# Sink values loaded late, and x of batches 2 to 4 transposed by the DMA crossbar in place of TensorE

## The chip, the cores and the metric

The kernel runs on one core of a Trainium2 chip. The metric is the device time of one execution in microseconds; smaller is better. A core has TensorE (PE: matmuls into PSUM, with weight loads that overlap them), VectorE (DVE), ScalarE (ACT), GpSimd (POOL) and SyncE (SP), which here only issues transfers. SyncE's transfers go through a hardware queue (q1 in the profile), GpSimd's through a software queue (q0); 16 DMA engines serve both. Each engine runs its instructions in their written order and waits on semaphores.

## The reference

An attention layer whose heads are of two kinds, followed by a wave-like mixing layer. B is 4, H 8, S 768, D 64, so the model width is 512; 4 sink positions, a window of 64.

```
scores = q @ k.T / sqrt(D)                       # per batch and head, 768 x 768
retrieval heads (0, 2, 6): causal mask
streaming heads (1, 3, 4, 5, 7): causal and (key < 4 or query - key < 64)
x = softmax(scores) @ v                          # (B, S, 512), heads side by side
theta = x @ w_theta
y = w_tok_r @ (x * cos(theta)) + w_tok_i @ (x * sin(theta))
u = x + y
out = u + relu(u @ w_ch)
```

## The kernel before, in words

All matmuls run in bf16. A batch has an attention part and a mixing part. Attention: q and k of head pairs are transposed on TensorE (`turn_qk`, line 251) and copied to SBUF by ScalarE or VectorE (`keep_qk`); scores S go to PSUM (`multiply`, line 322), ScalarE takes the exponential into P or, for streaming heads, P_st (lines 338 to 349), VectorE masks P_st (line 358) and GpSimd the diagonal blocks of P. The value matmuls (`values`, line 409, tile pav) of a block row i of 128 queries multiply these with v (tile vt), with a copy of v that is shifted by half a block (vx), and with the values of the sinks (vs). A column of ones in each gives the softmax sum, and `normalize` (VectorE, lines 414 and 416) writes a row of x.

Mixing: x is transposed four blocks at a time on TensorE (`turn_x`, line 421) into PSUM and copied into xT (`keep_x`, line 424: ScalarE in batch 1, VectorE in batches 2 to 4). `theta` (line 432) multiplies xT with w_theta, ScalarE takes cosine and sine (`wave`, tiles ct and st), VectorE multiplies x with the cosine (`z_real`, tile zr, line 442) and GpSimd, or VectorE for part of batch 1, x with the sine (`z_imag`, zi, line 445). `mix` (line 455, tile py) applies w_tok_r and w_tok_i, `make_u`, `turn_u`, `keep_u`, `channel` (line 474, pc) and `finish` (line 478) make the output, and SP stores it (line 481).

Values reach the core through SP: `load_v` (line 218) loads a head pair in two transfers into one of four staging buffers st_v; `cast_v` (line 222) makes vt, `shift_v` (lines 228 and 229 in batch 1, 232 and 233 later) makes vx. The sink values come by `sink_values` (line 244), five transfers for two batches at a time into the one buffer vs_f, and a VectorE cast (line 698) into vs. GpSimd issues the loads of q, k and the weights, with a cast from float.

No loop sets the order of the instructions. Each piece of work is a `Step` with an engine, an assumed duration, the steps it comes after, and the buffer slots it takes and gives back. `Plan.order` simulates the steps with these numbers and emits them by their simulated start; an engine takes the ready step with the longest path behind it. So a changed cost or dependency may move instructions anywhere. Real waits come from the tiles that instructions read and write. The plan's slots of note: score banks "s" 2 (also taken by pav and theta), transposition banks "x" 2, staging "st_v" 4.

Of the kernel before, what the change touches and what calls it, by code (L numbers as in the profile page):

```python
# [31 lines left out]
class Plan:  # L32
# [3 lines left out]

    LATENCY = {"PE": (230, 0), "ACT": (190, 60), "DVE": (120, 60), "POOL": (150, 60), "SP": (50, 0), "DMA": (2000, 0)}
    SWITCH = {"PE": 95, "ACT": 1300}  # L40
    HOLD = {"PE": 1500, "ACT": 8000}

# [11 lines left out]
    def order(self, free):  # L54
# [4 lines left out]
        rank = {}  # L59
# [4 lines left out]
        ready_at = {id(s): 0 for s in self.steps}  # L64
# [16 lines left out]
        while events:  # L81
            now = events[0][0]
            while events and events[0][0] <= now:
                _, _, done = heapq.heappop(events)
                if done is not None:
                    for g in done.give:
                        holding[id(g)] -= 1
                        if holding[id(g)] == 0:
                            slots[g.take] += 1
            for e in engines:  # L90
                if free.get(e, 0) > now:
                    continue
                best = None
                for s in ready.get(e, ()):
                    if ready_at[id(s)] > now or (s.take and slots[s.take] < 1):
                        continue
                    value = -ready_at[id(s)] if e == "DMA" else rank[id(s)] + s.bias
                    if s.mode and s.mode != mode.get(e):
                        value -= self.HOLD.get(e, 0)
                    if best is None or value > best[0]:  # L100
                        best = (value, s)
                if best is None:
                    continue
                s = best[1]
                ready[e].remove(s)
                t = now
                if s.mode and s.mode != mode.get(e):
                    if mode.get(e):
                        t += self.SWITCH.get(e, 0)
                    mode[e] = s.mode  # L110
                if s.take:
                    slots[s.take] -= 1
                s.start, s.end = t, t + s.ns
                out.append(s)
                lat = self.LATENCY[e]
                free[e] = s.end
                heapq.heappush(events, (s.end, count, None))
                heapq.heappush(events, (s.end + lat[0], count + 1, s))
                heapq.heappush(events, (s.end + lat[1], count + 2, None))
                count += 3  # L120
                for n in later[id(s)]:
                    waiting[id(n)] -= 1
                    ready_at[id(n)] = max(ready_at[id(n)], s.end + lat[n.eng == e])
                    if waiting[id(n)] == 0:
                        ready.setdefault(n.eng, []).append(n)
                        heapq.heappush(events, (ready_at[id(n)], count, None))
                        count += 1
# [6 lines left out]
def kernel(  # L134
# [14 lines left out]
    nc = tc.nc  # L149
# [268 lines left out]
    def turn_x(b, i):  # L418
        pt = state["ptx", b, i] = ps_x.tile([128, 1024], BF16, tag="x", name="pt")
        for kk in range(KD):  # L420
            nc.tensor.transpose(pt[:, kk * 128:(kk + 1) * 128], state["x", b][:, i, kk * 128:(kk + 1) * 128], ident)  # L421

    def keep_x(b, i):
        (nc.scalar.copy if b == 0 else nc.vector.tensor_copy)(state["xT", b][:, :, i * 128:(i + 1) * 128], state.pop(("ptx", b, i))[:, :DM].rearrange("p (k t) -> p k t", k=KD))

# [117 lines left out]

    cleared = [add(eng, ns, lambda n=n: clear(n)) for n, (eng, ns) in enumerate((("DVE", 900), ("POOL", 1300), ("DVE", 600), ("POOL", 1300)))]
    landed = {}
    gate = [add("DMA", ns, None) for ns in (2600, 2400, 4800)]
    for n in range(4):
        for what in "qk":
            landed[what, 0, n] = gate[min(n, 2)]
# [36 lines left out]
    def v_steps(b):  # L586
        for n in range(4):
            if b == 0:
                issue = add("DVE", 200, lambda n=n: load_v(0, n, kT[n // 2]), [kept["k", 0, n // 2]], take="st_v")
                land = add("DMA", 2000, None, [issue])  # L590
            else:
                issue = add("SP", 1500, lambda b=b, n=n: load_v(b, n), [cast[b - 1, n], xk[b - 1, 5]], take="st_v")
                land = add("DMA", 2000, None, [issue])
            old = [s for key, s in av.items() if key[0] == b - 1] if b else [cleared[1]]
            cast[b, n] = add("DVE" if b == 0 else "POOL", 570 if b == 0 else 830, lambda b=b, n=n: cast_v(nc.gpsimd if b else nc.vector, b, n), [land] + old, give=[issue])
            for x, h in enumerate(PAIRS[n]):
                if not IS_RETR[h]:
                    shift[b, h] = add("POOL", 960, lambda b=b, n=n, x=x: shift_v(nc.gpsimd, b, n, x), [cast[b, n]], give=[issue])

    def attention_steps(b):  # L600
        got = {}
# [24 lines left out]
        for i in range(NB):  # L626
            need = [sunk[b][1], sink_done[b // 2]] if i else []
            n = 0
            for h in range(H):
                pn = [x for x in range(4) if h in PAIRS[x]][0]  # L630
                need.append(cast[b, pn])
                if IS_RETR[h]:
                    need += [got[h, j, i] for j in range(i + 1)]
                    n += i + 1
                else:
                    need += [got[h, None, i], shift[b, h]]
                    n += 3 if i else 2
            av[b, i] = add("PE", n * 31 + 30, lambda b=b, i=i: first_values(b, i), need, take="s", mode="128")
            old = [ud[b - 2, t] for t in range(NB)] if b > 1 else []
            norm[b, i] = add("DVE", 850, lambda b=b, i=i: normalize(b, i), [av[b, i]] + old, give=[av[b, i]])  # L640
            xt[b, i] = add("PE", 224, lambda b=b, i=i: turn_x(b, i), [norm[b, i]], take="x", mode="128")
            old = [th[b - 1, t, y] for t in (0, 2, 4) for y in range(2)] if b else []
            xk[b, i] = add("DVE" if b else "ACT", 400 if b else 480, lambda b=b, i=i: keep_x(b, i), [xt[b, i]] + old, give=[xt[b, i]])
        for i in (0, 2, 4):
            for y in range(2):
# [12 lines left out]
    def mlp_steps(b):  # L658
        for t in range(NB):
# [6 lines left out]
            ch[b, t] = add("PE", 864, lambda b=b, t=t: channel(b, t), [uk, channel_w], take="m", give=[uk], mode="128")  # L666
            fin = add("DVE", 680, lambda b=b, t=t: finish(b, t), [ch[b, t]], take="ot", give=[ch[b, t], ud[b, t]], bias=URGE)
            st = add("SP", 100, lambda b=b, t=t: store(b, t), [fin])
            add("DMA", 900, None, [st], give=[fin])

    turn_steps(0)
    v_steps(0)
# [19 lines left out]
    weights(4, 2, [])  # L692
    ones_done = add("POOL", 600, sink_ones, [cleared[3]])
    sink_done = []
    for half in range(2):
        first = add("SP", 500, lambda half=half: sink_values(2 * half), [cleared[2]] + sink_done)
        land = add("DMA", 100, None, [first])
        sink_done.append(add("DVE", 480, lambda half=half: nc.vector.tensor_copy(vs[:32, 2 * half:2 * half + 2, :, :D], vs_f), [land, cleared[3], ones_done]))
    attention_steps(0)
    for b in range(1, B):  # L700
        turn_steps(b)
        v_steps(b)
        if b + 1 < B:
            load_steps(b + 1, [kept[what, b - 1, n] for what in "qk" for n in range(4)])
        attention_steps(b)
        mlp_steps(b - 1)
# [46 lines left out]
```

## Time and profile before

| | us |
|---|---|
| median of 3 runs | 226.41 (226.37 to 229.37) |
| profiled execution | 229.25 |
| its span, first to last instruction | 227.5 |
| PE busy | 195.2 (86%) |
| DVE busy | 122.2 (54%) |
| ACT busy | 120.2 (53%) |
| POOL busy | 101.1 (44%) |

The profiled execution is one run, taken with the hardware profiler; durations below are its own. Views of the trace name an instruction by its source line, its engine and its tiles, and say how long an engine stood idle before it and what it waited for. A busy time by stretch adds up an engine's instructions in a piece of the span; PEclk is the granted clock of TensorE there. Where a stretch is full on one engine, work taken off it shortens the run; where it isn't, the wait that ends last counts.

### The profile page before, as it was taken

What the parts mean: (1) busy time and instruction counts of PE and PEld (TensorE: products, weight loads), DVE (VectorE), ACT (ScalarE), POOL (GpSimd) and SP (SyncE); (2) the same over time, 40 slices, a digit from 0 to 9 for tenths busy, and PEclk for the clock granted to TensorE, in tenths of its full rate; (3) what the DMA queues carried; (4) which work ended last, traced back from release to release, by engine and by line L of the source; (5) the groups of instructions that cost most, each with busy time, mean ns of one, the idle gap of its engine ahead of it and who ended that gap; (6) DMA issues with size and microseconds to landing.
All of it is one profiled execution on the core that took longest, in us unless ns stands there. A gap on an engine that the chain in (4) does not pass through costs nothing.

```text
span 227.5 us, 5040 instructions
## 1 busy us (share of the span) xinstructions
PE 195.2 (86%) x2124; PEld 113.1 (50%) x2124; DVE 122.2 (54%) x203; ACT 120.2 (53%) x156; POOL 101.1 (44%) x180
## 2 busy tenths in 40 slices
PE   0688549968997899999999999959999999689990
PEld 0555339634554577544553468525544575234440
DVE  6327815389542168479135168495451764974341
ACT  2477402793499960184777563644977526703120
POOL 7955992072488300349852200299835000780000
PEclk9999999999999589999999999997999999999997
DMA  6994599999994934902103000960012000210303
GB/s 76 164 210 108 80 174 213 192 200 199 195 209 98 202 55 118 208 14 81 49 0 127 14 0 3 242 178 0 3 48 94 3 3 0 92 49 0 138 0 140
DMA packets 39759, 22.63 MB, mean 99 GB/s; under 512 B 25912, under 2 KB 36664, under 8 KB 39736
## 3 DMA queue, kind: packets, MB, share of 16 engines
q0 software_dynamic: 11072, 9.70, 27.4%
q1 hardware_dynamic: 28664, 12.61, 21.2%
q8 instruction: 16, 0.26, 0.5%
q14 instruction: 7, 0.06, 0.1%
HBM read 25.71 MB, written 6.29 MB: 141 GB/s over the span
## 4 chain that ended last, share of the span: by engine, by line
PE 72%; DVE 8%; ACT 6%; DMA 5%; POOL 3%; issue 3%; POOLq 1%; SPq 1%; DVEq 0%; ACTq 0%
PE py L455 26%; PE pav L409 9%; PE ps L322 9%; PE pc L474 7%; PE pt L251 7%; PE ps L432 6%; DVE zr L442 5%; POOL zi L445 3%; PE pt L421 3%; PE pt L464 3%; DMA vs_f<-in_v_dram 2%; PE pt L494 2%; DMA kb<-in_k_dram 2%; ACT P L341 2%; ACT P_st L338 1%
## 5 line engine op out<-in xcount | busy, mean ns | idle before, releaser
L455 PE MATMUL py<-zr,wtokTr 128*128 128x512 bf16 x144 | 39.7, 385 | 6.3 <-DVE zr L442 6.3
L445 POOL TENSOR_TENSOR zi<-x,st 128x512 bf16<-128x512 bf16 x20 | 27.8, 1421 | 25.2 <-ACT st L439 19.8
L455 PE MATMUL py<-zi,wtokTi 128*128 128x512 bf16 x144 | 38.5, 379 | 0.1
L459 DVE TENSOR_TENSOR u<-x,py 128x512 bf16<-128x512 bf16 x24 | 16.5, 687 | 36.1 <-PE py L455 36.1
L322 PE MATMUL ps<-qT,kT 64*64 64x128 bf16 (+6 forms) x380 | 26.7, 266 | 6.5 <-ACT P L341 2.2
L442 DVE TENSOR_TENSOR zr<-x,ct 128x512 bf16<-128x512 bf16 x24 | 27.9, 1197 | 1.3 <-ACT ct L437 1.3
L468 ACT COPY uT<-pt 128x512 bf16<-128x512 bf16 x24 | 13.9, 586 | 26.5 <-PE pt L464 26.4
L478 DVE SCALAR_TENSOR_TENSOR ot<-pc,u 128x512 f32<-128x512 f32 x24 | 16.5, 688 | 16.4 <-PE pc L474 15.1
L222 POOL CAST vt<-st_v 128x768 bf16<-128x768 f32 x12 | 10.2, 856 | 33.3 <-DMA st_v<-in_v_dram 33.1
L322 PEld LDWEIGHTS <-kT 64*64 64x64 bf16 (+1 forms) x380 | 13.6, 113 | 21.7 <-issue 17.1
L200 POOL TENSOR_SCALAR_AFFINE_SELECT P<-P 128x256 bf16<-128x256 bf16 (+1 forms) x48 | 16.5, 365 | 17.2 <-ACT P L346 6.6
L474 PE MATMUL pc<-w_ch_sb,uT 128*128 128x512 bf16 x96 | 24.0, 380 | 0.0
L432 PE MATMUL ps<-w_theta_sb,xT 128*128 128x512 bf16 x96 | 23.2, 379 | 0.9 <-ACT st L439 0.9
L437 ACT ACTIVATE ct<-ps,half_pi 128x1024 f32<-128x1024 f32 x12 | 13.0, 1113 | 20.1 <-PE ps L432 19.5
L341 ACT ACTIVATE P<-ps 128x1024 bf16<-128x1024 f32 (+2 forms) x24 | 21.2, 923 | 4.5 <-PE ps L322 4.5
L455 PEld LDWEIGHTS <-wtokTr 128*128 128x128 bf16 x144 | 12.6, 98 | 19.7 <-issue 7.6
L258 ACT COPY qT<-pt 128x768 bf16<-128x768 bf16 x14 | 11.0, 802 | 18.7 <-PE pt L251 18.5
L455 PEld LDWEIGHTS <-wtokTi 128*128 128x128 bf16 x144 | 13.3, 98 | 14.9 <-issue 0.4
L358 DVE TENSOR_TENSOR P_st<-P_st,m_stream 128x512 bf16<-128x512 bf16 (+2 forms) x24 | 12.8, 543 | 14.7 <-ACT P_st L349 10.5
L409 PE MATMUL pav<-vx,P_st 128*128 128x65 bf16 x120 | 17.4, 207 | 3.5 <-POOL vx L228 3.5
L409 PE MATMUL pav<-vt,P 128*128 128x65 bf16 x252 | 16.1, 207 | 1.8 <-DVE x L416 1.8
L409 PE MATMUL pav<-vt,P_st 128*128 128x65 bf16 x120 | 17.5, 208 | 0.0
(73 smaller groups left out, 323.8 us busy)
## 6 DMA issues: line engine op xcount, KB each, us to landing
st_v<-in_v_dram SPq DMA_DIRECT2D x32, 192.0 KB
out_dram<-ot SPq DMA_DIRECT2D x24, 256.0 KB
qb<-in_q_dram POOLq DMA_DIRECT2D x3, 768.0 KB, 10.8
kb<-in_k_dram POOLq DMA_DIRECT2D x3, 768.0 KB, 15.4
wtok<-in_moe_w_tok_r_dram POOLq DMA_DIRECT2D x3, 384.0 KB, 11.9
wtok<-in_moe_w_tok_i_dram POOLq DMA_DIRECT2D x3, 384.0 KB, 12.7
w_theta_sb<-in_moe_w_theta_dram POOLq DMA_DIRECT2D x1, 512.0 KB, 5.7
w_ch_sb<-in_moe_w_ch_dram POOLq DMA_DIRECT2D x1, 512.0 KB, 21.1
```

The source lines that it names most:

```text
L200: nc.gpsimd.affine_select(out=t, in_=t, compare_op=ALU.is_ge, fill=0.0, base=base, pattern=pattern, channel_multiplier=cm)
L251: nc.tensor.transpose(pt[64 * x:64 * x + 64, j * 128:(j + 1) * 128], state[what, b][:, h, j * D:(j + 1) * D], ident)
L322: nc.tensor.matmul(ps[half, yy, c:c + w], l, r, start=True, stop=True, skip_group_check=True)
L341: nc.scalar.activation(P.rearrange("p (y c) -> p y c", y=2), ps[:, :, :w0], AF.Exp, scale=scale)
L409: nc.tensor.matmul(o, l, r, start=(m == 0), stop=True, skip_group_check=True)
L432: nc.tensor.matmul(ps[:, y], state["xT", b][:, kk, (i + y) * 128:(i + y + 1) * 128], w_theta_sb[:, kk], start=(kk == 0), stop=(kk == KD - 1))
L442: nc.vector.tensor_tensor(state["zr", b][:, i + y], state["x", b][:, i + y], state["ct", b, i][:, y], ALU.mult)
L445: (nc.vector if eng == "DVE" else nc.gpsimd).tensor_tensor(state["zi", b][:, i + y], state["x", b][:, i + y], state["st", b, i][:, y], ALU ...
L455: nc.tensor.matmul(py, wtokT[n][:, s, t * 128:(t + 1) * 128], z[:, s], start=(g == 0 and m == 0), stop=(g == 2 and m == 3))
L459: nc.vector.tensor_tensor(u, state["x", b][:, t], state.pop(("py", b, t)), ALU.add)
L474: nc.tensor.matmul(pc, uT[:, kk], w_ch_sb[:, kk], start=(kk == 0), stop=(kk == KD - 1))
L478: nc.vector.scalar_tensor_tensor(ot, state.pop(("pc", b, t)), 0.0, state.pop(("u", b, t)), ALU.max, ALU.add)
```

## The change

Three things change. The second half of the sink values (batches 3 and 4) is planned after the value loads of batch 2, and its load waits in the plan for the first cast of batch 2's values; before, both halves came at the start. In batches 2 to 4, `turn_x` and `keep_x` give way to one DMA transpose per block row, issued by SP (`send_x`: SBUF x, 128 x 512, to SBUF xT, four blocks of 128 x 128). In batch 1 the shifted copies vx are made by VectorE in place of GpSimd. With these, numbers of the plan change: the arrival of the first q and k loads, the cost of a value load and of a sink load on SP, and a separate DMA lane ("DMAH") for transfers that SP issues. Lines after the new function move by 3, later ones by up to 11 (698 becomes 705).

```diff
+    def send_x(b, i):
+        nc.sync.dma_start_transpose(state["xT", b][:, :, i * 128:(i + 1) * 128], state["x", b][:, i])
...
-    gate = [add("DMA", ns, None) for ns in (2600, 2400, 4800)]
+    gate = [add("DMA", ns, None) for ns in (4300, 2000, 6000)]
...
-                issue = add("SP", 1500, lambda b=b, n=n: load_v(b, n), [cast[b - 1, n], xk[b - 1, 5]], take="st_v")
-                land = add("DMA", 2000, None, [issue])
+                issue = add("SP", 700, lambda b=b, n=n: load_v(b, n), [cast[b - 1, n], xk[b - 1, 5]], take="st_v")
+                land = add("DMAH", 2000, None, [issue])
...
-                    shift[b, h] = add("POOL", 960, lambda b=b, n=n, x=x: shift_v(nc.gpsimd, b, n, x), [cast[b, n]], give=[issue])
+                    shift[b, h] = add("POOL" if b else "DVE", 960 if b else 340, lambda b=b, n=n, x=x: shift_v(nc.gpsimd if b else nc.vector, b, n, x), [cast[b, n]], give=[issue])
...
+            old = [th[b - 1, t, y] for t in (0, 2, 4) for y in range(2)] if b else []
+            if b:
+                issue = add("SP", 800, lambda b=b, i=i: send_x(b, i), [norm[b, i]] + old)
+                xk[b, i] = add("DMAH", 900, None, [issue])
+                continue
             xt[b, i] = add("PE", 224, lambda b=b, i=i: turn_x(b, i), [norm[b, i]], take="x", mode="128")
...
-    for half in range(2):
-        first = add("SP", 500, lambda half=half: sink_values(2 * half), [cleared[2]] + sink_done)
-        land = add("DMA", 100, None, [first])
-        sink_done.append(add("DVE", 480, lambda half=half: nc.vector.tensor_copy(vs[:32, 2 * half:2 * half + 2, :, :D], vs_f), [land, cleared[3], ones_done]))
+    def sink_steps(half, after):
+        first = add("SP", 1500, lambda: sink_values(2 * half), [cleared[2]] + after)
+        land = add("DMAH", 300, None, [first])
+        sink_done.append(add("DVE", 480, lambda: nc.vector.tensor_copy(vs[:32, 2 * half:2 * half + 2, :, :D], vs_f), [land, cleared[3], ones_done]))
+
+    sink_steps(0, [])
     attention_steps(0)
     for b in range(1, B):
         turn_steps(b)
         v_steps(b)
+        if b == 1:
+            sink_steps(1, [sink_done[0], cast[1, 0]])
```

What the plan makes of it is seen in the order of the instructions. SP's queue, from its start to the stores of batch 2 (vs_f is the sinks' buffer, st_v the staging of values, ot a result), before:

```order
L244 DMA vs_f<-in_v_dram 4x2x64 x5
L218 DMA st_v<-in_v_dram 128x6x64 x8
L244 DMA vs_f<-in_v_dram 4x2x64 x5
L218 DMA st_v<-in_v_dram 128x6x64 x8
L481 DMA out_dram<-ot 128x512 x3
L218 DMA st_v<-in_v_dram 128x6x64 x8
L481 DMA out_dram<-ot 128x512 x7
```

The same place after:

```order
L244 DMA vs_f<-in_v_dram 4x2x64 x5
L218 DMA st_v<-in_v_dram 128x6x64 x16
L244 DMA vs_f<-in_v_dram 4x2x64 x5
L424 DMA_TRANSPOSE xT<-x 128x4x128
L484 DMA out_dram<-ot 128x512 x2
L218 DMA st_v<-in_v_dram 128x6x64 x8
L424 DMA_TRANSPOSE xT<-x 128x4x128
L484 DMA out_dram<-ot 128x512
L424 DMA_TRANSPOSE xT<-x 128x4x128 x4
L484 DMA out_dram<-ot 128x512 x4
```

The second sink load now stands behind the value loads of batches 1 and 2, and transposes stand among stores and value loads.

On VectorE, the second cast of the sinks before, ahead of the first normalization of batch 1:

```order
L698 CAST vs<-vs_f 32x10x64
L222 CAST vt<-st_v 128x2x6x64
L358 TENSOR_TENSOR P_st<-P_st,m_stream 128x2x4x64 x2
L358 TENSOR_TENSOR P_st<-P_st,m_stream 128x4x64
L698 CAST vs<-vs_f 32x10x64
L414 RECIPROCAL r<-pav 128x8
L416 TENSOR_TENSOR x<-pav,r 128x2x4x64
```

And after, where it stands now, in the mixing part of batch 1:

```order
L445 TENSOR_TENSOR zr<-x,ct 128x512 x2
L448 TENSOR_TENSOR zi<-x,st 128x512 x3
L705 CAST vs<-vs_f 32x10x64
L501 COPY wtokTi<-pt 128x6x128
L358 TENSOR_TENSOR P_st<-P_st,m_stream 128x2x4x64
L462 TENSOR_TENSOR u<-x,py 128x512
```

It moved from before the first x to behind the last z products of batch 1.

On TensorE, scores of batch 2 (ps, with the numbers of the buffers) before:

```order
L322 MATMUL ps_1132<-qT0_88,kT0_92 128x128
L322 LDWEIGHTS kT0_92
L322 MATMUL ps_1141<-qT0_88,kT0_92 128x256
L322 LDWEIGHTS kT0_92
L322 MATMUL ps_1141<-qT0_88,kT0_92 128x256
L322 LDWEIGHTS kT1_93
L322 MATMUL ps_1147<-qT1_89,kT1_93 128x256
```

And after, the end of such a score tile:

```order
L322 MATMUL ps_1045<-qT0_88,kT0_92 128x256
L322 LDWEIGHTS kT0_92
L322 MATMUL ps_1045<-qT0_88,kT0_92 128x256
L458 LDWEIGHTS wtokTi_87
L458 MATMUL py_1012<-zi_463,wtokTi_87 128x512
```

Before, score tiles of batch 2 follow one another; after, token-mixing matmuls of batch 1 stand between them.

## Rows read from the trace of the kernel before

**Rows 1.** The page's busy time, share of the span and instructions, TensorE.

```profile
PE 195.2 (86%) x2124; PEld 113.1 (50%) x2124; DVE 122.2 (54%) x203; ACT 120.2 (53%) x156; POOL 101.1 (44%) x180
```

**Rows 2.** Busy time by stretch: length, engines' busy us (instructions), PEclk, DMA share, GB/s.

```profile
24.50:34.60 10.10, 4.77 (x53) 3.45 (x52) 4.89 (x11) 1.28 (x2) 9.65 (x16) 1.00 0.95 153
34.60:40.50 5.90, 5.90 (x93) 5.90 (x94) 3.00 (x8) 1.45 (x3) 0.95 (x2) 1.00 1.27 211
45.50:56.00 10.50, 7.58 (x67) 4.14 (x67) 9.63 (x12) 7.23 (x8) 5.47 (x6) 1.00 1.19 199
71.00:82.50 11.50, 8.60 (x112) 5.93 (x107) 4.61 (x11) 9.27 (x16) 4.73 (x11) 0.70 0.94 139
82.50:147.00 64.50, 64.02 (x744) 36.50 (x742) 35.94 (x67) 36.36 (x46) 22.36 (x38) 1.00 0.26 71
147.00:158.00 11.00, 8.29 (x80) 4.36 (x75) 9.45 (x9) 5.48 (x7) 10.47 (x12) 0.84 0.43 115
158.00:197.00 39.00, 38.86 (x441) 21.32 (x440) 20.43 (x38) 24.80 (x33) 13.05 (x27) 1.00 0.09 35
197.00:201.00 4.00, 1.72 (x8) 0.73 (x8) 4.00 (x4) 1.98 (x2) 4.00 (x4) 1.00 0.00 0
```

**Rows 3.** Waits, 20 to 36 us: us in total, times, longest.

```profile
DVE vs L698 <- DMA vs_f<-in_v_dram: 5.2, 1, 5.2
...
PE pav L409 <- POOL vx L228: 3.5, 3, 1.5
...
PE pav L409 <- DVE x L416: 1.8, 1, 1.8
```

**Rows 4.** Chain that ended last, near 28 us: start, us, what.

```profile
27.75 5.37 DMA vs_f<-in_v_dram
```

**Rows 5.** DMA queues, 29 to 62 us, and one load issued there with its landing.

```profile
q0 software_dynamic: 4771, 4.84, 88.7%
q1 hardware_dynamic: 6197, 1.55, 31.0%
...
kb<-in_k_dram POOLq DMA_DIRECT2D x2, 768.0 KB, 16.6
```

**Rows 6.** TensorE's timeline: start, us, line, tiles, count.

```profile
38.13 0.74 PE L409 MATMUL pav<-vt,P 128*128 128x65 bf16 x10
...
40.53 0.42 PE L409 MATMUL pav<-vt,P 128*128 128x65 bf16 x8
...
138.10 0.48 PE L409 MATMUL pav<-vt,P 128*128 128x65 bf16 x10
```

**Rows 7.** Waits, 70 to 83 us, the longest of TensorE's.

```profile
PE ps L322 <- ACT P L341: 1.4, 3, 0.5
```

**Rows 8.** GpSimd's timeline, one of the shifted copies of batch 1.

```profile
29.10 0.50 POOL L228 COPY vx<-vt 64x390 bf16<-64x390 bf16 x1
```

**Rows 9.** SP's timeline, its eight value loads for batches 2, 3 and 4.

```profile
28.09 21.26 SPq L218 DMA_DIRECT2D st_v<-in_v_dram  x8
...
86.94 6.70 SPq L218 DMA_DIRECT2D st_v<-in_v_dram  x8
...
142.39 5.41 SPq L218 DMA_DIRECT2D st_v<-in_v_dram  x8
```

**Rows 10.** Chain that ended last, a transposition of x and theta behind it.

```profile
141.15 0.22 PE pt L421 x4
141.38 1.73 PE ps L432 x8
```

**Rows 11.** Line 424, VectorE's copies of xT: ns min/median/max.

```profile
L424 DVE COPY xT<-pt x18: 411/416/425, 88.1 to 190.9; 128x512 bf16<-128x512 bf16 x18
```

**Rows 12.** Waits of the whole run, TensorE for zr.

```profile
PE py L455 <- DVE zr L442: 6.3, 5, 1.4
```

**Rows 13.** Chain that ended last: a normalization, and a store at the end.

```profile
33.85 0.70 DVE x L416
...
221.11 2.30 DMA out_dram<-ot
```

More of the change, by code (lines that the diff above doesn't have):

```diff
@@ L32 @@
 class Plan:
-    LATENCY = {"PE": (230, 0), "ACT": (190, 60), "DVE": (120, 60), "POOL": (150, 60), "SP": (50, 0), "DMA": (2000, 0)}
+    LATENCY = {"PE": (230, 0), "ACT": (190, 60), "DVE": (120, 60), "POOL": (150, 60), "SP": (50, 0), "DMA": (2000, 0), "DMAH": (2000, 0)}
     SWITCH = {"PE": 95, "ACT": 1300}
@@ L96, in order @@
                         continue
-                    value = -ready_at[id(s)] if e == "DMA" else rank[id(s)] + s.bias
+                    value = -ready_at[id(s)] if e[:3] == "DMA" else rank[id(s)] + s.bias
                     if s.mode and s.mode != mode.get(e):
@@ L589, in v_steps @@
                 issue = add("DVE", 200, lambda n=n: load_v(0, n, kT[n // 2]), [kept["k", 0, n // 2]], take="st_v")
-                land = add("DMA", 2000, None, [issue])
+                land = add("DMAH", 2000, None, [issue])
             else:
-                issue = add("SP", 1500, lambda b=b, n=n: load_v(b, n), [cast[b - 1, n], xk[b - 1, 5]], take="st_v")
-                land = add("DMA", 2000, None, [issue])
+                issue = add("SP", 700, lambda b=b, n=n: load_v(b, n), [cast[b - 1, n], xk[b - 1, 5]], take="st_v")
+                land = add("DMAH", 2000, None, [issue])
             old = [s for key, s in av.items() if key[0] == b - 1] if b else [cleared[1]]
@@ L640, in attention_steps @@
             norm[b, i] = add("DVE", 850, lambda b=b, i=i: normalize(b, i), [av[b, i]] + old, give=[av[b, i]])
+            old = [th[b - 1, t, y] for t in (0, 2, 4) for y in range(2)] if b else []
[3 more added lines that the diff above has]
+                continue
             xt[b, i] = add("PE", 224, lambda b=b, i=i: turn_x(b, i), [norm[b, i]], take="x", mode="128")
-            old = [th[b - 1, t, y] for t in (0, 2, 4) for y in range(2)] if b else []
             xk[b, i] = add("DVE" if b else "ACT", 400 if b else 480, lambda b=b, i=i: keep_x(b, i), [xt[b, i]] + old, give=[xt[b, i]])
@@ L668, in mlp_steps @@
             st = add("SP", 100, lambda b=b, t=t: store(b, t), [fin])
-            add("DMA", 900, None, [st], give=[fin])
+            add("DMAH", 900, None, [st], give=[fin])
     turn_steps(0)
```

## The prediction

> **What bounds the kernel now.** I read the page's busy times first, then the busy times by stretch, then the waits and the chain in each stretch that is not full. TensorE is busy for 86% of the span [rows 1], and by stretch the share splits in two kinds [rows 2]. From 82.5 to 147 us it is busy for 64.02 of 64.50 us and from 158 to 197 for 38.86 of 39.00: there every instruction taken off TensorE shortens the run by what it took. In between lie four holes: 24.5 to 34.6 (4.77 busy of 10.10), 45.5 to 56 (7.58 of 10.50), 71 to 82.5 (8.60 of 11.50, mean granted clock 0.70) and the ends of batches 3 and 4, 147 to 158 (8.29 of 11.00, clock 0.84) and 197 to 201 (1.72 of 4.00). Batches are counted from 1 here, as in the name of the change.
>
> The first hole has two causes in the waits [rows 3]. Three times a value matmul waits for GpSimd's shifted copy vx, 3.5 us in all; and VectorE stands 5.2 us in front of the second cast of the sink values, with the normalizations of the first batch behind it in its order, so that TensorE runs out of score banks and waits 1.8 us for an x. The chain shows what VectorE waits for: five transfers of sink values, 2 KB each by their shape (4 x 2 x 64 floats), of which the last takes 5.37 us to land [rows 4]. What makes so little slow is the queue: from 29 to 62 us the software queue holds 88.7% of the engines and the hardware queue, on which they travel, 31.0% [rows 5].
>
> The clock hides a second loss. Ten value matmuls in a row take 0.74 us at 38.13 and 0.48 us at 138.10 [rows 6]; by their starts that is 55 against 32 ns each, for 65 columns, the lower and the upper of the two levels (1.2 and 2.4 GHz), although the page prints 1.00 for both. TensorE reaches the upper one at 40.5 us, after being busy without a gap from 34.6, and falls again between 71 and 82.5 after waits for ScalarE's exponentials [rows 2, 7].
>
> **The change part by part.** The sum is made against the profiled execution, 229.25 us with a span of 227.5, which is 2.84 above the median of 226.41.
>
> A, the start. The second half of the sink values moves behind the value loads of batch 2, and its cast moves on VectorE from ahead of the first normalization to behind the z products of batch 1. This frees up to 1.8 us of TensorE. The shifts of batch 1 move to VectorE and with that 3.5 us of waits for GpSimd go; the price is ten copies on VectorE, by GpSimd's row 0.50 us for the longer of a pair [rows 8], which fit into the 5.2 us that VectorE loses now, but stand ahead of the last masks, so I charge 1.0 of them. Value loads of batch 2 no longer queue behind the sinks: SP issues them from 28.09 on, and eight of them hold it for 21.26 us there, against 6.70 and 5.41 us in the later, quiet stretches [rows 9]. Issued as soon as a staging buffer is free, they can run before the software queue fills the engines. With fewer gaps the upper clock comes earlier too; thirty value matmuls at 32 in place of 55 ns are 0.7 us. The planner's new arrival times for the first loads only put the same scores of batch 1 in another order, which I cost at nothing; if that order is worse, it eats from the lower bound. Sum: 3.5 + 1.8 - 1.0 + 0.7 = 5.0 us gained, between 2.0 (the masks bind in place of the shifts) and 6.5 (twice that clock gain and hidden shifts).
>
> B, the third hole. Now TensorE issues the scores of batch 2 in one go and waits for score banks behind ScalarE [rows 7]; in the new order they lie between the token-mixing matmuls py of batch 1. The hole holds 11.50 - 8.60 = 2.9 us idle, and a clock of 0.70 over 11.50 us costs 3.4. I take 4.0 of 6.3 us as gained; bounds 0 and 6.3.
>
> C, the transposes. Eighteen groups of four leave TensorE. In the chain a group holds it for 0.22 us [rows 10], so 18 x 0.22 = 4.0 us, all in batches 2 to 4, whose last stages lie in the full stretches. Eighteen copies of 0.42 us leave VectorE [rows 11], 7.5 us, which I cost at nothing: VectorE waits for TensorE there.
>
> D, the ends of batches 3 and 4. The holes there (2.7 us idle and 1.8 of clock, then 2.3) are waits for the first zr (five such waits in the run, 6.3 us [rows 12]) while GpSimd's zi run beside them. The new order has scores and turned q and k of the next batch to put there in batch 3, and more py in batch 4. I take 2.0 of 6.8; bounds 0 and 6.8.
>
> E, the new waits. SP now carries eighteen transposes in order with stores and value loads, and one that waits for its x holds those behind it; VectorE then waits for an ot buffer. A transpose needs its x, then t on the queue, then landing, and up to five follow each other behind the last normalizations. Nothing in the trace is a crossbar transfer. Bounds for t are SP's rows: 5.41/8 = 0.68 us below, 21.26/8 = 2.66 above [rows 9]; I take 6.70/8 = 0.84, since the engines are mostly free after 82.5 us (DMA share 0.26 [rows 2]), and a landing of 2.30 us, that of a store at the end [rows 13]. With 0.9 for the normalization (0.70 [rows 13] and a reciprocal before it) the last x is turned 5 x 0.84 + 2.30 + 0.9 = 7.4 us after its matmuls, at worst. In the new order some 32 matmuls of 512 columns, at 1.73/8 = 0.216 us each [rows 10] about 7 us, lie between the last value matmul and the theta group that reads that x. The stall is 0.4 us a batch, 1.2 in all; with one more wait the size of a mean zr wait (1.3 us [rows 12]) E is 2.5 us lost, from 0 upwards to the second rival's price.
>
> What is given up for this is a row of blocks turned in 0.22 us of TensorE and a 0.42 us copy [rows 10, 11]. The Trainium skill, VectorE: DVE Perf Modes, The three transpose paths, speaks against the change: it gives 1309 ns for a 128x128 crossbar transpose against 390 ns on TensorE, and its rules say to use TensorE where a PSUM destination will do. If four blocks cost four times that on the queue, t would be 5.2 us, an estimate from that page, and the time about 280 us by the formula of the second rival; no row here shows a crossbar transfer either way.
>
> Sum: -5.0 - 4.0 - 4.0 - 2.0 + 2.5 = -12.5 us. From the profiled time that is 216.75. If the 2.84 us that it lies above the median are the clock loss of the third hole, median runs have less to gain and 226.41 - 9.7 = 216.7 comes out; if they are spread, 213.9. I take **215.5 us**.
>
> **The rivals.** *The start stays where the DMA engines put it.* The loads of batch 1's weights and batch 2's q and k are the same bytes; kb takes 16.6 us to land there [rows 5], and the new order turns q and k of batch 2 ahead of the last theta group, so TensorE would stand at them instead, and the late sink cast would stall VectorE again behind its z products. For it: the engines are full from 29 to 62 us. Against it: the value loads, eight of 128 x 6 x 64 floats, can leave that stretch for the idle time before it. A is lost and half to all of B: 220.5 + 2.0 to 220.5 + 4.0, so 222.5 to 224.5 us, no change.
>
> *The crossbar path is late.* TensorE waits at theta for xT in every batch. Without new waits the time is 213.0; each batch adds 5t + 2.30 + 0.9 - 7. At t = 2.66 that is 9.5 us a batch and 241.5 us. It ends slower by over 2% (230.9) from t = 2.0 us on. For it: eight value loads cost 2.66 each when the engines are shared, and stores that wait for VectorE stand ahead of transposes on SP. Against it: from 82.5 us on the engines are mostly idle.
>
> *More than forecast.* If the clock stays up from 34 us on and D's holes fill, the rest of A, B and D and no E give up to 11 us more; half of that is 210.
>
> **How the numbers follow.** Forecast, 210 to 221.9: 0.70. More than that, below 210: 0.08. The start stays: 0.14. The crossbar path is late: 0.08. About 2% is what a measurement of this kernel tells from no change, 221.9 to 230.9. Faster 0.78, same 0.14, slower 0.08. The range goes from 209.5 to 223.5: it leaves out the late path, the upper part of the rival of no change, and the tail below.
>
> **What would show it.** A: the last value matmul of batch 1 ends by 37 us (41.4 now), with no sink wait on VectorE's list and the eight loads of batch 2 issued in under 10 us. B: no clock fall near 75 us. C: transposes by line 421 in batch 1 alone, 24 of 96. E: SP's row for a transpose under 1 us, and TensorE's waits for a DMA of xT under 3 us in all. Wrong if a transpose holds SP for over 2 us, or if TensorE waits for q and k of batch 2.

## The result, and the profile after

The changed kernel takes 220.11 us in the median of four runs (218.84 to 221.34), the kernel before 227.82 on the same chip; the ratio is 0.966, with a 95% interval of 0.9555 to 0.9765. The forecast was 215.5 with a range of 209.5 to 223.5: the sign and the range hold, and the gain (7.7 us) is some 60% of the 12.5 that were added up. Times here and below are medians of all executions, while a ratio leaves out those of either kernel that took over 1.5% longer than its fastest. The profiled execution took 221.34 us, the longest of the four, with a span of 219.6; times within it are compared with the 229.25 and 227.5 of the kernel before.

The page's busy line, which answers to [rows 1]:

```profile
PE 188.1 (86%) x2025; PEld 106.6 (49%) x2052; DVE 119.4 (54%) x195; ACT 119.6 (54%) x156; POOL 98.1 (45%) x170
```

TensorE's share is the same; the span (7.9 us shorter) fell with its work (7.1 us less). This trace has 2052 weight loads but records of only 2025 matmuls, so some 27 matmuls are missing and TensorE's busy time is a little too low. Where it is not full now is read from the busy times by stretch (length, then the engines in the page's order, granted clock, DMA share, GB/s), as in [rows 2] but with other borders:

```profile
24.50:36.00 11.50, 8.25 (x182) 7.69 (x181) 7.96 (x19) 3.57 (x5) 4.52 (x6) 0.80 1.21 204
36.00:40.00 4.00, 3.95 (x29) 2.45 (x28) 0.90 (x2) 2.46 (x5) 2.00 (x4) 0.88 1.27 192
40.00:50.00 10.00, 6.97 (x115) 4.53 (x115) 7.41 (x9) 9.31 (x11) 8.05 (x11) 1.00 1.20 204
50.00:62.00 12.00, 9.43 (x69) 4.98 (x65) 7.16 (x9) 6.75 (x10) 10.27 (x15) 0.72 0.39 58
62.00:74.00 12.00, 11.74 (x148) 6.34 (x148) 4.74 (x10) 9.08 (x14) 1.56 (x5) 1.00 1.32 204
74.00:82.00 8.00, 6.38 (x95) 4.25 (x94) 4.13 (x10) 4.91 (x7) 1.88 (x5) 0.96 1.16 228
82.00:86.00 4.00, 3.95 (x73) 3.84 (x72) 3.04 (x7) 0.00 (x0) 0.49 (x1) 0.66 1.14 257
145.00:155.00 10.00, 7.28 (x76) 3.78 (x75) 6.02 (x8) 9.98 (x12) 7.45 (x8) 1.00 0.15 54
155.00:212.90 57.90, 57.05 (x489) 29.03 (x497) 27.86 (x46) 26.16 (x36) 13.68 (x20) 1.00 0.20 56
```

The old third hole (71 to 82.5) is filled: 62 to 74 us has 11.74 of 12. The hole at the end of batch 4 is gone as well. But 74 to 86 us has become one (10.33 busy of 12, clock 0.66 at the end), and 40 to 62 us, which had a hole before, is worse (16.40 busy of 22, clock 0.72 in the later part). The kernel before, from 40 to 62 us:

```profile
40.00:62.00 22.00, 18.96 (x197) 11.13 (x197) 15.17 (x21) 13.35 (x17) 7.92 (x13) 1.00 1.22 197
```

TensorE's waits in the whole run (us in total, times, longest) do not name GpSimd's vx any more, VectorE's do not name the sink values (both were in [rows 3]), and nothing on TensorE waits for xT. Four of TensorE's:

```profile
PE py L458 <- DVE zr L445: 3.9, 4, 1.2
PE pt L497 <- DMA wtok<-in_moe_w_tok_r_dram: 1.9, 1, 1.9
PE ps L322 <- ACT st L442: 1.7, 1, 1.7
PE pav L409 <- DVE x L416: 1.5, 1, 1.5
```

In SP's timeline (start, us, what, count) the sixteen value loads of batches 1 and 2 now go in one go from 8.71 us, where the second eight began at 28.09 [rows 9]; the sink values follow them, and five transposes hold the queue for 7.47 us:

```profile
8.71 23.75 SPq L218 DMA_DIRECT2D st_v<-in_v_dram  x16
32.50 1.81 SPq L244 DMA_DIRECT2D vs_f<-in_v_dram  x5
...
132.52 7.47 SPq L424 DMA_TRANSPOSE xT<-x  x5
```

What made 40 to 62 us worse in this execution stands in the timelines of GpSimd, ScalarE and TensorE (in brackets the idle time before a row and what ended it). GpSimd's order has the fetch of a further block of the token weights, which waits 3.39 us for a wtok buffer, and all casts of batch 2 ahead of the first two zi of batch 1:

```profile
41.52 0.70 POOL L490 DMA_DIRECT2D wtok<-in_moe_w_tok_r_dram  x1 [3.39 <-PE pt L497]
...
50.09 3.16 POOL L448 TENSOR_TENSOR zi<-x,st 128x512 bf16<-128x512 bf16 x2
...
53.29 1.02 ACT L442 ACTIVATE st<-ps 128x1024 f32<-128x1024 f32 x1 [2.97 <-POOL zi L448]
...
54.36 0.90 PE L322 MATMUL ps<-qT,kT 64*128 64x256 bf16 x4 [1.70 <-ACT st L442]
```

Read downwards: the late zi hold a buffer that ScalarE's third st needs, and that st holds the PSUM bank (theta's, of the same pool) that TensorE's next scores need. In the kernel before, GpSimd made the first two zi 6.9 us after the last normalization of batch 1 and ahead of the casts of batch 2; now they come 13.1 us after it (50.09 against 37.0). Before:

```profile
49.38 2.29 POOL L445 TENSOR_TENSOR zi<-x,st 128x512 bf16<-128x512 bf16 x2
...
58.61 0.83 POOL L222 CAST vt<-st_v 128x768 bf16<-128x768 f32 x1
```

The chain that ended last (start, us, what) shows the other place:

```profile
73.39 0.70 DVE ot L481
...
74.11 5.38 DMA out_dram<-ot
...
79.61 0.69 DVE ot L481
...
80.45 0.70 DVE x L416
...
81.20 1.44 PE pav L409 x24
```

There are two buffers for ot. The third ot of batch 1 waits 2.80 us for the first store, which takes 5.38 us from its issue on; the last such store of the run takes 2.04. In the whole run ot waits twice for a store, 3.9 us in all; in the kernel before it was one wait:

```profile
DVE ot L478 <- DMA out_dram<-ot: 1.4, 1, 1.4
```

VectorE's normalizations of batch 2 stand behind that ot, and TensorE's value matmuls behind those. From 66 to 82 us the software queue, with q and k of batches 3 and 4, holds 88.7% of the DMA engines, as it did over the sink values [rows 5]. That this load is what makes the store slow is read from these numbers, and no run tests it alone.

By the ends of the last normalization of each batch, read from VectorE's timeline (span times in us), this is where the time went:

| | batch 1 | batch 2 | batch 3 | batch 4 | 1 to 2 |
|---|---|---|---|---|---|
| before | 42.5 | 89.6 | 141.3 | 188.9 | 47.1 |
| after | 37.0 | 87.0 | 136.8 | 179.3 | 50.0 |

5.5 us are gained by the end of batch 1, 2.9 of them are lost again by the end of batch 2, and 6.9 come back by the end of batch 4. From there to the end of the last matmul it takes 2 us longer than before (35.5 against 33.5 us), and the span ends 7.9 us earlier. These are single executions; how much of the 2.9 us belongs to this one alone is taken up under the three buffers below.

### The profile page after: what moved, and what is told of

Read it like the earlier page. It is cut to its first block, busy times and chain, and to the rows that moved or that the text cites. A ratio compares the mean times of both kernels' runs of the same rounds, so it can differ in the third digit from the quotient of the medians.

```text
span 219.6 us, 4889 instructions
## 1 busy us (share of the span) xinstructions
PE 188.1 (86%) x2025; PEld 106.6 (49%) x2052; DVE 119.4 (54%) x195; ACT 119.6 (54%) x156; POOL 98.1 (45%) x170
## 4 chain that ended last, share of the span: by engine, by line
PE 66%; DMA 10%; DVE 8%; POOL 6%; ACT 5%; issue 4%; DVEq 0%; POOLq 0%
PE py L458 28%; PE ps L322 8%; PE ps L435 7%; PE pav L409 7%; PE pc L477 5%; DMA wtok<-in_moe_w_tok_r_dram 5%; DVE zr L445 4%; DMA out_dram<-ot 3%; PE pt L251 3%; PE pt L467 3%; DVE ot L481 3%; PE pt L497 2%; DMA kb<-in_k_dram 2%; POOL zi L448 1%; ACT qT L258 1%
## 5 line engine op out<-in xcount | busy, mean ns | idle before, releaser
L458 PE MATMUL py<-zr,wtokTr 128*128 128x512 bf16 x136 | 38.4, 383 | 4.8 <-DVE zr L445 3.9
L448 POOL TENSOR_TENSOR zi<-x,st 128x512 bf16<-128x512 bf16 x20 | 27.2, 1386 | 22.6 <-PE py L458 19.4
L322 PEld LDWEIGHTS <-kT 64*64 64x64 bf16 (+1 forms) x380 | 13.0, 108 | 22.7 <-issue 17.1
L477 PE MATMUL pc<-w_ch_sb,uT 128*128 128x512 bf16 x88 | 22.8, 380 | 0.8 <-issue 0.6
L458 PEld LDWEIGHTS <-wtokTr 128*128 128x128 bf16 x144 | 12.5, 98 | 16.9 <-issue 6.1
L358 DVE TENSOR_TENSOR P_st<-P_st,m_stream 128x512 bf16<-128x512 bf16 (+2 forms) x24 | 11.9, 501 | 10.0 <-ACT P_st L338 6.9
L409 PE MATMUL pav<-vt,P 128*128 128x65 bf16 x252 | 15.6, 204 | 1.8 <-DVE x L416 1.5
L416 DVE TENSOR_TENSOR x<-pav,r 128x512 bf16<-128x512 f32 x24 | 16.6, 692 | 0.9
L409 PE MATMUL pav<-vx,P_st 128*128 128x65 bf16 x120 | 16.1, 201 | 0.0
L409 PE MATMUL pav<-vt,P_st 128*128 128x65 bf16 x120 | 16.1, 201 | 0.0
```

The lines of the kernel that those rows point to most:

```text
L322: nc.tensor.matmul(ps[half, yy, c:c + w], l, r, start=True, stop=True, skip_group_check=True)
L409: nc.tensor.matmul(o, l, r, start=(m == 0), stop=True, skip_group_check=True)
L416: nc.vector.tensor_tensor(dst, av[:, :, :, :D], r.unsqueeze(3).to_broadcast([128, 2, 4, D]), ALU.mult)
L448: (nc.vector if eng == "DVE" else nc.gpsimd).tensor_tensor(state["zi", b][:, i + y], state["x", b][:, i + y], state["st", b, i][:, y], ALU ...
L458: nc.tensor.matmul(py, wtokT[n][:, s, t * 128:(t + 1) * 128], z[:, s], start=(g == 0 and m == 0), stop=(g == 2 and m == 3))
L477: nc.tensor.matmul(pc, uT[:, kk], w_ch_sb[:, kk], start=(kk == 0), stop=(kk == KD - 1))
```

## The experiments

Ratios are to the kernel before, from the runs beside it, with a 95% interval. Its median beside them lay between 227.81 and 229.43 us, so ratios compare better than times.

### What are the transposes worth?

**The rest without them.** The branch that sends x to the crossbar is left out of the changed kernel, and the planner orders the steps anew:

```diff
-            if b:
-                issue = add("SP", 800, lambda b=b, i=i: send_x(b, i), [norm[b, i]] + old)
-                xk[b, i] = add("DMAH", 900, None, [issue])
-                continue
```

> The changed kernel with the transposes of x of batches 2 to 4 back on TensorE and the copies back on VectorE; the late sink values and all other edits stay, and the planner orders the steps anew. Theory: taking the transposes off TensorE is worth its full 4.0 us, because xT is nowhere waited for, so this kernel loses them: 223 to 225.5 us, about 0.98 of the kernel before, with a ratio of 1.01 to 1.025 to the changed one. Rival: the gain is the start's and the new order's alone, and the transposes lay in time that TensorE had to spare: 219 to 221.5 us.

Measured: 221.34 us, ratio 0.9676 (0.961 to 0.9742). That is the rival's number. As the change stands (0.966), its transposes are worth nothing that can be measured beside the rest of it. One thing they do bring is seen by stretch: without them the third hole stays,

```profile
62.00:74.00 12.00, 9.43 (x130) 6.30 (x129) 3.88 (x8) 11.88 (x18) 6.18 (x14) 0.86 1.25 226
```

so the closing of the third hole (step B) came with the order that the planner finds for the crossbar, not with the early start. (Two runs below that keep this order, with three buffers for ot, have 9.43 there too.)

**They alone.** The kernel before with that branch and what it needs (`send_x` and the lane DMAH for its transfers), and nothing else:

```diff
+            if b:
+                issue = add("SP", 800, lambda b=b, i=i: send_x(b, i), [norm[b, i]] + old)
+                xk[b, i] = add("DMAH", 900, None, [issue])
+                continue
```

> The kernel before with only the transposes of x of batches 2 to 4 moved to the crossbar; sinks and the start as before. Theory: TensorE is busy 4.0 us less and never waits for xT, so 222.5 to 224.5 us against 226.4 to 229.4. Rival (the transposes hidden, the start does it all): 226 to 229 us, no change that can be measured.

Measured: 228.04 us, ratio 1.004 (0.9993 to 1.0087): the rival's again. But the planner moved much else, so this does not tell work from order. The next run does.

**Exchanged in place.** The planner still plans a transpose on TensorE and a copy on VectorE, at the old costs and so in the old order; what is emitted is the crossbar transfer, where the copy stood:

```diff
-lambda b=b, i=i: turn_x(b, i), [norm[b, i]]
+lambda b=b, i=i: None if b else turn_x(b, i), [norm[b, i]]
...
-lambda b=b, i=i: keep_x(b, i), [xt[b, i]]
+lambda b=b, i=i: (send_x if b else keep_x)(b, i), [xt[b, i]]
```

> The kernel before with every engine's order as the planner set it there, and only this exchanged in place: where VectorE copied xT of batches 2 to 4 out of PSUM, SyncE now issues the crossbar transpose, and TensorE's transposes of x are left out. The planner costs are untouched, so nothing else moves. Theory (work): TensorE's 4.0 us go in full, 222.5 to 224.5 us. Rival (path): the products with theta were planned to follow the transposes closely, and the way over SyncE and the DMA engines takes about 3 us longer than over TensorE and VectorE, so TensorE waits up to 3 us for xT in each of three batches, and what it wins in work it loses in waits: 227 to 231 us.

Measured: 233.18 us, ratio 1.0205 (1.0154 to 1.0257). The rival (path) holds, and the loss is larger than it said. The profiled execution took 236.15, 3 us above the median; TensorE's waits, SP's timeline and TensorE's:

```profile
PE ps L435 <- DMA xT<-x: 7.0, 4, 4.0
...
144.97 1.22 SPq L424 DMA_TRANSPOSE xT<-x  x1
...
147.85 1.70 PE L435 MATMUL ps<-w_theta_sb,xT 128*128 128x512 bf16 x4 [4.04 <-DMA xT<-x]
```

4.0 us of work saved and 7.0 of waits make 3.0 lost; the medians say 4.9, and the other 2 are not settled. The matmul that waits starts 147.85 - 146.19 = 1.66 us after SP has finished the transpose; for this landing the forecast took 2.30.

**The same exchange beside late sink values**, in the order of the first run, with two buffers for ot and then with three. First with two:

> The same exchange in place in the kernel of the first run (late sink values and the other edits, transposes on TensorE, 221.3 us there), its order untouched. Theory (work): 4.0 us less, 216.5 to 218.5 us. Rival (path): TensorE waits for xT and the transposes of batch 2 stand on SyncE ahead of eight value loads of batch 3: 220 to 224 us.

Measured: 220.02 us, ratio 0.9634 (0.9595 to 0.9674), against 0.9676 (0.961 to 0.9742) without the crossbar: 0.4% less, with intervals that overlap. Three executions took 219.43 to 220.38 us, at the lower end of the rival's range and just below it. The profiled one took 363.58, with TensorE's matmuls of 512 columns at 668 to 680 ns in the mean of a group, where they take some 380 in the other traces, at a recorded clock of 1.0; why is open, and its profile says nothing on the exchange. Then the first run with a third buffer, as the reference for the exchange:

```diff
-        ot = state["ot", b, t] = work.tile([128, DM], F32, tag="ot", name="ot")
+        ot = state["ot", b, t] = work.tile([128, DM], F32, tag="ot", name="ot", bufs=3)
```

> The kernel of the first run (late sink values and the other edits, transposes of x on TensorE) with three buffers for ot, its order untouched. In that run one ot waited 5.3 us for a store. Theory (path): the transposes are worth little once the waits for stores are gone too, and this comes within 1% of the changed kernel with three ot (216.3 us): 216 to 218.5 us. Rival (work): only with the stores' waits gone do TensorE's 4.0 us count, and this is 219.5 to 221.5 us.

Measured: 222.15 us, ratio 0.9682 (0.964 to 0.9724), on the rival's side. Without the crossbar a third buffer brings nothing (0.9676 with two), though one ot waited 5.3 us there: that wait did not set the time.

> The kernel of the run beside it (late sink values, three ot) with the transposes of x of batches 2 to 4 exchanged in place for crossbar ones, its order untouched. Work: 4.0 us less than that run. Path: within 1.5 us of it, since TensorE waits for xT up to 4 us where an order planned for the short path is kept; in the same exchange in the kernel before TensorE waited 6.8 us for xT in all.

Measured: 219.72 us, ratio 0.9577 (0.9536 to 0.9617), 2.43 us less than the run beside it. TensorE's wait for xT in it is

```profile
PE ps L435 <- DMA xT<-x: 1.7, 2, 1.2
```

and 4.0 - 1.7 = 2.3. So here the transposes taken off TensorE are worth what they took, less what TensorE then waits for xT; in the exchange in the kernel before, the same sum fell 2 us short. Both theories were half of it. What the eighteen copies that leave VectorE bring is not separated from this.

### What is the start worth?

**Late sink values alone.**

```diff
-    for half in range(2):
-        first = add("SP", 500, lambda half=half: sink_values(2 * half), [cleared[2]] + sink_done)
...
+    sink_steps(0, [])
...
+        if b == 1:
+            sink_steps(1, [sink_done[0], cast[1, 0]])
```

> The kernel before with only the second five sink value loads moved behind the first value load and cast of batch 2 (the planner orders the rest anew at the old costs). Theory: the late sink values are what gives the gain of the start and so nearly all of the change: VectorE has no wait for them, SyncE issues batch 2's sixteen value loads early, 220.5 to 223.5 us. Rival: the shifted copies on VectorE and the new planner numbers are needed for it, since in the kernel before the value products of batch 1 wait 3.5 us for GpSimd's vx: 225 to 229 us.

Measured: 227.39 us, ratio 0.9932 (0.9886 to 0.9978). The theory falls: this edit, the first in the name of the change, gives 0.7% (`sink_steps` is that of the change, with its cost of a sink load). SP does issue sixteen loads at once, VectorE has no sink wait, but the value matmuls of batch 1 still wait for GpSimd, 4.2 us against 3.5 [rows 3]:

```profile
8.06 18.15 SPq L218 DMA_DIRECT2D st_v<-in_v_dram  x16
...
PE pav L409 <- POOL vx L228: 4.2, 4, 1.5
```

**Shifted copies of batch 1 on VectorE, alone.**

```diff
-                    shift[b, h] = add("POOL", 960, lambda b=b, n=n, x=x: shift_v(nc.gpsimd, b, n, x), ...
+                    shift[b, h] = add("POOL" if b else "DVE", 960 if b else 340, lambda b=b, n=n, x=x: shift_v(nc.gpsimd if b else nc.vector, b, n, x), ...
```

> The kernel before with only the shifted copies of batch 1 (vx) moved from GpSimd to VectorE; sink values and transposes as before. Theory: the waits for vx go (3.5 us) but the sink values' wait on VectorE and the late loads of batch 2 stay, so 225 to 228.5 us. Rival: the waits for vx were what held the start, and 221 to 224 us come out without the late sink values.

Measured: 226.42 us, ratio 0.9937 (0.9908 to 0.9967), the theory's number. The last normalization of batch 1 ends at 37.7 us, 4.8 earlier; by batch 2 (86.8) 2.8 are left.

**Both, at the old planner costs** (but for the sink load's).

> The kernel before with both edits of the start, the late sink values and the shifted copies of batch 1 on VectorE, and nothing else (old planner costs, transposes on TensorE). Each alone gave 0.993 to 0.994. Theory: each alone leaves the other's wait at the same place, so together they give the start's whole gain: 221 to 223.5 us. Rival: it takes the new planner costs (first loads of q and k, value loads on SyncE, stores) to turn the start's gain into time: 224 to 227 us.

Measured: 226.48 us, ratio 0.9844 (0.9787 to 0.9901), the rival's number. Batch 1's last normalization ends at 36.4 us, 6.1 earlier, so the two edits do add up there (4.8 + 1.1). The rival looked to the new costs for the rest, and rightly: the first run has both edits as well, at the new planner costs (first loads, value loads on SP, a lane of its own for SP's transfers), and reaches 0.9676. The step from 0.9844 to 0.9676, as large as both edits together, is those costs, which change nothing but the order. (Their intervals, to 0.9787 and from 0.9742 on, do not meet.) Which of the costs it is was not tested.

### Where was the gain lost?

**Three buffers for ot** in the changed kernel, as in the diff above, every engine's order untouched.

> The changed kernel with three buffers for ot in place of two, the order of all instructions unchanged. Theory: part of the gain of the start is lost between 74 and 86 us, where VectorE's third ot waits 2.8 us for a store that takes 5.4 us to land, with the normalizations of batch 2 behind it and TensorE's clock at the lower level afterwards; and about 2.7 us in the last stage, where ot waits for stores. With three buffers both waits go: 215.5 to 218 us. Rival: the work behind the ot is held by something else as well (the queue of loads is still full), so the wait moves to the next ot or to the normalizations: 219 to 221.5 us.

Measured: 216.32 us, ratio 0.9462 (0.9405 to 0.9519). The theory's number. VectorE's third ot now waits 0.50 us, for TensorE, in place of 2.80 for a store:

```profile
72.64 0.69 DVE L481 SCALAR_TENSOR_TENSOR ot<-pc,u 128x512 f32<-128x512 f32 x1 [0.50 <-PE pc L477]
```

Batch 2's last normalization ends at 79.45, 7.5 us earlier than in the changed kernel. Not all of that is the third buffer. 1.2 us are there at the end of batch 1, and 4.7 at the end of the first x of batch 2 (67.78 against 72.45), before the third ot, where both kernels still run the same instructions in the same order. That part is a difference of two executions: here the scores that waited 1.70 us for st do not wait, and the clock stays up from 50 to 62 us (1.00 against 0.72). From TensorE's timeline and the busy times by stretch:

```profile
52.23 0.54 PE L322 MATMUL ps<-qT,kT 64*128 64x256 bf16 x4
...
50.00:62.00 12.00, 10.66 (x96) 5.48 (x93) 6.79 (x12) 9.22 (x14) 9.31 (x15) 1.00 0.77 116
```

So 3.4 us of the 50.0 from batch 1 to batch 2 in the table above are no effect of the buffers, and they are more than the 2.9 us lost there. The 2.8 us that are left of the 7.5 are the wait that went.

**The first zi earlier.** With the planned order in hand, three steps are moved, on GpSimd alone:

```diff
+    early = [zs[0, "i", 0], zs[0, "i", 1]]
+    late = fetched[0, 4]
+    order = [s for s in order if s not in early and s is not late]
+    at = 1 + max(order.index(s) for s in early[0].after)
+    order[at:at] = early + [late]
```

(`fetched` holds the fetches of the token weights by their number.)

> The changed kernel with one difference, in GpSimd's order: the first two zi of batch 1 and the fetch of the fifth block of the token weights stand behind nine casts of batch 2 in the order zi, zi, fetch, so that the wait of 3.4 us for a wtok buffer goes from ahead of zi. Theory: the start's gain is lost between 40 and 62 us since zi comes late, ScalarE's third st waits 3.0 us for its buffer, the scores of batch 2 wait for ScalarE, and the clock falls to its lower level: zi begins near 46 in place of 50.1, the first product of the token weights begins 3 us earlier, and the time is 215.5 to 218 us. Rival: another wait in the same stretch (the copies of q and k of batch 2 on ScalarE, or the start of batch 2's loads) ends as late, so 219 to 221.5 us.

Measured: 219.63 us, ratio 0.9564 (0.9478 to 0.965); the interval reaches into both expectations (the time lies in the rival's range). GpSimd's row and VectorE's say what happened:

```profile
42.75 2.29 POOL L448 TENSOR_TENSOR zi<-x,st 128x512 bf16<-128x512 bf16 x2 [3.24 <-issue]
...
75.72 0.69 DVE L481 SCALAR_TENSOR_TENSOR ot<-pc,u 128x512 f32<-128x512 f32 x1 [5.52 <-DMA out_dram<-ot]
```

zi come 7.3 us earlier (1.7 of them from batch 1's end, which the edit does not touch) and the second ot 6.6 us (69.07 for 75.68), but the third then waits 5.52 us for its store where it waited 2.80 and is 3.9 us earlier: 2.7 us of what one place gave, the next one took.

**Both.**

> The changed kernel with both three buffers for ot (216.3 us alone) and GpSimd's first two zi ahead of the fetch and two casts (219.6 us alone). Theory: the earlier zi brought the stretch of 40 to 62 us 2.9 us forward, and it was lost again since the third ot then met a store that took even longer; with three buffers it is kept: 212.5 to 215 us. Rival: what comes earlier meets the q and k loads of batch 3 and 4 and waits for those: 215.5 to 217.5 us.

Measured: 213.68 us, ratio 0.932 (0.9273 to 0.9368). The theory's number, the fastest of all and clear of the changed kernel and of three ot alone (0.932 against 0.9462). By stretch, the two bad places:

```profile
40.00:50.00 10.00, 6.75 (x116) 4.26 (x118) 6.97 (x10) 8.76 (x11) 6.99 (x11) 1.00 1.22 207
50.00:62.00 12.00, 11.90 (x108) 6.01 (x110) 5.48 (x11) 9.83 (x15) 7.08 (x12) 1.00 0.97 146
62.00:74.00 12.00, 11.71 (x203) 8.28 (x204) 8.12 (x16) 8.95 (x13) 2.66 (x8) 1.00 1.32 201
74.00:82.00 8.00, 7.95 (x87) 4.42 (x85) 4.92 (x10) 0.59 (x1) 2.98 (x5) 1.00 1.07 247
82.00:86.00 4.00, 2.57 (x15) 1.19 (x15) 0.08 (x1) 1.87 (x2) 3.69 (x8) 1.00 0.61 159
```

The granted clock is 1.00 in all five stretches, where the changed kernel had 0.72 and 0.66. The next hole is at 82 us, and it is the crossbar's: SP has eight value loads of batch 3 ahead of five transposes of batch 2, and TensorE waits.

```profile
69.56 10.17 SPq L218 DMA_DIRECT2D st_v<-in_v_dram  x8
...
81.76 5.16 SPq L424 DMA_TRANSPOSE xT<-x  x4
...
PE ps L435 <- DMA xT<-x: 2.1, 2, 1.4
```

Issuing those transposes ahead of the value loads was not tried.

## Why the prediction held, and where it was off

That the time came out in the range is luck in part. The first run, without the transposes and the order found for them, already has 0.9676: A and the planner's numbers alone gave 7.4 us, nearly all of the 7.7 measured. B, C, D and E, forecast at 7.5 together, added nothing that could be measured. The planner's numbers, which the sum costed at nothing, gave some 4 us in their place.

**A, the start (-5.0): right in size, partly wrong in cause.** The last value matmul of batch 1 ends at 36.0 us, under the 37 named, and its normalization 5.5 us earlier. The shifted copies give 4.8 of it and the late sink values 1.1, about the 3.5 and 1.8 of the sum. By themselves both edits bring 3.6 us of it to the end of the run (1.6%; the interval is 1.0 to 2.1%). What the step missed is the planner's new numbers: costed at nothing, they give as much again. One sign named for this step failed, the eight loads of batch 2 issued in under 10 us: the last of the sixteen alone holds SP for 9.04 us, and the second eight take some 15.

**B, the third hole (-4.0): the step that failed.** The old hole did close, and no clock fall is left near 75 us. Yet from batch 1 to batch 2 the profiled execution lost 2.9 us, where B and a third of C stood for a gain of 5.3; even without the 3.4 us by which the run with three ot, in the same order, is faster ahead of its third ot, it would have gained only 0.5. The waits that took its place are two: GpSimd's late zi, of which the prediction has nothing, and the ot behind a store. The second it names in E ("VectorE then waits for an ot buffer"), as a result of transposes that hold SP, and prices with one mean zr wait of 1.3 us. SP was not what held it; the store went out at once and took 5.38 us among the loads, just as the sink values did in [rows 4], a row that the prediction read and used only for the start. Mending the waits for stores is worth 2.0% (0.966 to 0.9462), and the earlier zi behind that another 1.4% (0.9462 to 0.932). With both gone this stretch takes 41.6 us (35.24 to 76.82) in place of 47.1: the gain is 5.5, so the forecast's 5.3 was about what the order could give.

**C, the transposes (-4.0): right as a term, and hidden in the sum.** In place, 4.0 less 1.7 of waits stood against 2.4 measured. As the change stands nothing of it could be measured, because what the planner's new order for the crossbar won (C and B) went into the two new waits; with three ot, the crossbar and its order are worth 0.9462 against 0.9682, some 5 us.

**D, the ends of batches 3 and 4 (-2.0): the right sign.** From the end of batch 2 to that of batch 4 the kernel gains 6.9 us, two thirds of C included (2.7, an estimate), and gives 2 back after it; 6.9 - 2.7 - 2.0 leaves about 2.2. No run tested this, and the share of each batch was not separated.

**E, the new waits (+2.5): mis-sized, and in the wrong place.** A transpose holds SP for 1.22 us (median of 18), above the 0.84 taken and the 1 us named. TensorE nevertheless waits for xT nowhere, since the cover is more than the 7 us assumed: the last x of batch 3 is done at 136.8 us, and the theta group that reads it begins at 148.2. In the order of before, where there is no such cover, the same transposes cost 7.0 us of waits; in the run of the crossbar alone, which the planner ordered for the longer path, 2.7. So the mechanism of the rival of the late crossbar is real, and the order decides what it costs.

In rows, a transpose of four 128x128 blocks takes 1.22 us of SP, and 2.9 us from its issue to a matmul that waits for it. The Trainium skill, VectorE: DVE Perf Modes, The three transpose paths, has 1309 ns for one block, from which the prediction drew 5.2 us as an estimate; these runs do not bear that estimate out, and the measurement decides.

**The rivals.** "The start stays" fell with batch 1's 36.0 us. "The crossbar path is late" did not come about in the changed kernel, where no matmul waited for xT. "More than forecast" did not come about either; with both waits mended the kernel takes 213.7 us, against the 210 of that rival.

## What to carry to other kernels

Work taken off the bound engine brought less here than its duration, once even a loss, since the longer path added waits; exchange it in place, in a fixed order, to see both numbers. A change that makes one stage earlier moves its stores and loads into another stage's traffic: look there for a buffer count of two in front of a transfer that was short until now, and ask what stands behind the waiting instruction on its engine. Where a planner sets the order, run the edit at fixed order too: here the planner's numbers moved the time as much as the edits. And before a stretch of one profile is explained, look for the same stretch in a run that has the same instructions there: part of the loss may be that execution's.

## What the hardware showed that was not expected

In the changed kernel a crossbar transpose holds SP for 1196 to 2182 ns, median 1218. The two that were issued at 72.6 and 84.1 us, among the loads (DMA share 1.31 and 1.23 around them), took 1288 and 1262, so they hardly minded the load, while a single value load on the same queue took 390 to 9037 ns, median 623. A store that takes 2.04 us at the end takes 5.38 with the software queue at 88.7% of the engines. And a short wait of VectorE can cost TensorE its clock: behind the 2.8 us for the store TensorE stood 1.50 us for an x, and the granted clock was 0.66 from 82 to 86 us; without the wait it was 1.00 there. By medians three ot brought 3.8 us, about the 2.8 of that wait and the 1.1 of the other, at the end of the run.
